# Gated linear attention and two MLPs on one core: decay work passes two waits per mixing step, and squares queue behind the table functions

## The chip, the cores and the metric

The kernel runs on 1 core of a Trainium2 chip. The metric is the device time of one execution in microseconds (us). Before the change the median of 3 runs is 912.96 us (908.11 to 916.42). The profiled execution took 912.68 us, of which its trace covers a span of 910.9 us.

The engines are named as in the profile: PE is TensorE (its sequencer of weight loads is PEld), DVE is VectorE, ACT is ScalarE, POOL is GpSimd, SP is SyncE, which issues most DMAs.

## The reference

Inputs are 4 batches x 8 heads x 768 positions x 48 channels. The first part is a linear recurrence with a complex decay per position and channel; its output is fed through a token-mixing MLP, a channel MLP, a layer norm and a second channel MLP.

```python
mag = sqrt(a_re**2 + a_im**2);  s = minimum(mag, 0.999) / (mag + 1e-6)
a_re, a_im = a_re * s, a_im * s
for t in range(768):                     # per batch and head, state 48 x 48
    S_re, S_im = a_re*S_re - a_im*S_im + k[t] v[t]^T, a_re*S_im + a_im*S_re
    y[t] = q[t] @ S_re
x = y, heads side by side                # 4 x 768 x 384
u = x + (relu(x^T @ w_tok1) @ w_tok2)^T  # 768 -> 256 -> 768 over tokens
u = u + relu(u @ w_ch1) @ w_ch2          # 384 -> 1536 -> 384
out = u + relu(norm(u) * g @ m_ch1) @ m_ch2
```

## The kernel before

The recurrence is not stepped through. For each batch the decays are turned into cumulated magnitudes and angles, q and k are scaled by them, and each head becomes a few matmuls on chunks of 128 positions. So there are three kinds of work, each a Python generator, and a driver that takes turns between them:

- **Decay work** (`gen_E`, class `Piece`). A batch's 8 x 48 channels are 3 tiles of 128 partitions; each tile is worked in two pieces of 384 positions. A piece runs through the parts F (squares of both decay parts, L228, logarithms and exponentials, L198, magnitude), G (a scan), H (scaling of q and k), T1 (arctangent and a scan of the angle), T2 (sine and cosine) and T3 (products, L172 on VectorE, and the DMAs into the heads' stacked tiles `stk`, L338 and L339). The work is split over ScalarE (functions of `aj` and `t`) and VectorE (all recorded at L172). ScalarE holds one table of functions at a time: the helper `act` loads the logarithm table or the sine table (L196) when the kind changes and puts the first function of the new kind behind all functions of the old kind. `Piece.F` calls the squares directly, not through `act`, so nothing but its data says where they stand.
- **Heads** (`gen_P`). A head is transposes of k (L507), scores of 3 x 128 columns twice (L520), states (L547), outputs (L570 to L577 for heads of batches 3 and 4), with their evictions, splits into two 16-bit halves and sums of squares on ScalarE and VectorE. Three steps per head.
- **Mixing** (`gen_M`). Per batch: token mixing (`tok1`, two hid activations; `tok2`, six evictions at L721), then 4 passes of a channel MLP, 12 steps each. Each step is 9 matmuls 128x384 from `u`, one activation on ScalarE (L670, written to `hid`), its remainder on VectorE (L672), and 9 matmuls from `hid`. Token mixing of the next batch needs all eight heads of that batch.

The driver, at the end of `tile_kernel`, runs one mixing step, then `run_E(2200)`, then up to two head steps. `run_E` takes items of decay work until their costs sum to 2200 or until the generator yields "wait", a mark that the next item needs another engine's result. A piece has seven such marks, so a batch has 42, against 48 mixing steps. Heads are taken at most at half a step per mixing step, and not before the tile that they need. When 47 steps are done all heads of the next batch are run at once. Decay work of a tile also waits until a head has given up its `stk` tile. So decay work and heads of batch b+1 (and some decay work of b+2) lie beside the mixing of batch b.

What is written this way is then put into an order for each engine by a scheduler that follows data dependences and a timeline of its own; an instruction written late can stand early. Each engine works its own list strictly in that order.

There are 198 hid activations at L670 (48 in batch 1, 50 in each other batch), evenly spaced in the work; this document uses their number as a ruler. Numbers 49 and 50 are token mixing of batch 2, 99 and 100 of batch 3, 149 and 150 of batch 4.

Of the kernel before, what the change touches and what calls it, by code (L numbers as in the profile page):

```python
# [38 lines left out]
def tile_kernel(ctx: ExitStack, tc: tile.TileContext, a_in, qk_in, v_in, aq2_in, v2_in, wt_in, wm1_in, wm2_in, w64_in, g_in, c_in, out):  # L39
# [150 lines left out]
    def act(**k):  # L190
        s = "trig" if k["func"] in (AF.Sin, AF.Arctan) else "logs"
        if tab["set"] != s:
            with ExitStack() as gates:
                for x in tab["ops"]:
                    gates.enter_context(tc.issue_after(x))
                tab.update(set=s, load=A.preload_act_table_set(sets[s]).ins, ops=[])  # L196
        with tc.issue_after(tab["load"]):
            tab["ops"].append(A.activation(**k).ins)  # L198

    class Piece:  # L200

# [20 lines left out]
        def F(self):  # L222
            V = Rec()
            A_, B_, C_, D_ = self.t
            ar, ai, b = self.ar, self.ai, self.b
            c = 470 if self.n == 1 else 870
            yield "wait"
            A.activation(out=self.sq.rearrange("p (x s) -> p x s", x=2), in_=self.both, func=AF.Square)  # L228
            act(out=D_, in_=ar, func=AF.Ln)
            act(out=D_, in_=D_, func=AF.Exp, scale=-1.0, accum_out=acc())  # L230
            yield "wait"
            with after("go") if b == 1 and self.i == 0 and EGO else ExitStack():
                V.scalar_tensor_tensor(out=A_, in0=A_, scalar=TINY, in1=B_, op0=ALU.add, op1=ALU.add)
# [79 lines left out]
        def T3(self, qkt):  # L313
            V = Rec()
            A_, B_, C_, D_ = self.t
            b, i = self.b, self.i
            for y in (self.R, qkt):
                d = y[:, :, 2 * HB:2 * HB + 3]
                if self.hf == 0:
                    (A.activation(out=d, in_=self.h(self.dh), func=AF.Copy) if ACP else G.tensor_copy(out=d, in_=self.h(self.dh)))  # L320
                else:
                    if self.n == 2:
                        (A.activation(out=d[:, 0], in_=self.dh[:, 0:3], func=AF.Copy) if ACP else G.tensor_copy(out=d[:, 0], in_=self.dh[:, 0:3]))
                    (A.activation(out=d[:, self.n - 1, 0:2], in_=self.dh[:, 3 * self.n - 3:3 * self.n - 1], func=AF.Copy) if ACP else G.tensor_copy(out=d[:, self.n - 1, 0:2], in_=self.dh[:, 3 * self.n - 3:3 * self.n - 1]))
                    G.memset(d[:, self.n - 1, 2:3], 0.0)
            for k in range(self.n):
                hf = k if self.n == 2 else self.hf
                qk = qkt[:, k, 0:2 * HB].rearrange("p (x s) -> p x s", x=2)
                V.tensor_tensor(out=self.R[:, k, 0:2 * HB].rearrange("p (x s) -> p x s", x=2), in0=qk, in1=pair(self.h(A_)[:, k]), op=ALU.mult)
                yield 870  # L330
                V.tensor_tensor(out=qk, in0=qk, in1=pair(self.h(B_)[:, k]), op=ALU.mult)
                r = 0
                while r < P:
                    h, d0 = divmod(i * P + r, D)
                    m = min(D - d0, P - r)
                    if (b, h) not in stk:
                        stk[b, h] = shared() if b == 0 and h >= 2 else ap.tile([2 * D, 2, 2 * HB + 3], F32, tag="stk", name="stk", bufs=NSTK)
                    nc.sync.dma_start(out=stk[b, h][d0:d0 + m, hf], in_=self.R[r:r + m, k])  # L338
                    nc.sync.dma_start(out=stk[b, h][D + d0:D + d0 + m, hf], in_=qkt[r:r + m, k])  # L339
                    r += m  # L340
                yield 870

# [105 lines left out]
    def gen_P(alt):  # L448
# [30 lines left out]
        for n, (b, h) in enumerate(heads):  # L479
# [17 lines left out]
                dr = ap.tile([P, 2, DM], F16, tag="hid", name="dr", bufs=NHID).rearrange("p a b -> p (a b)").bitcast(F32)[0:2 * D, 0:NCH * D].rearrange("p (e c) -> p e c", c=NCH)  # L497
            else:
                dr = ap.tile([2 * D, D, NCH], F32, tag="dr", name="dr", bufs=1)
            A.activation(out=dr.rearrange("p e (y c) -> p e y c", y=2), in_=kq[:, :, 2 * HB:].unsqueeze(1).to_broadcast([2 * D, D, 2, 3]), func=AF.Copy)  # L500
            tr = ps_(2)
            Gv = tr[0:96, 0:NCH * D]
            y = None
            for half in range(2):
                if half == 0:
                    for c in range(5):
                        T.transpose(tr[:, c * 96:(c + 1) * 96], qc(c, 1), eye[0:96, 0:96])  # L507
                    kTc = A.activation(out=kT, in_=tr[:, 0:480].rearrange("p (c d) -> p c d", c=5), func=AF.Copy, scale=(VS * SS if n in YS else 1.0) / (QS if n in QZ else 1.0))
                    if n in YS:
                        vh = ap.tile([P, S], F32, tag="dw", name="vh", bufs=NDW).bitcast(F16)  # L510
                        Uh = vh[0:2 * D, 2 * NCH * D:4 * NCH * D].rearrange("p (x c e) -> p x c e", x=2, c=NCH)
                        Uc = U.rearrange("p e c -> p c e")
                        vh = vh[:, 0:2 * NCH * D].rearrange("p (x c e) -> p x c e", x=2, c=NCH)
                        m = YS.index(n)
                        A.activation(out=vh[:, 0], in_=v, func=AF.Copy, scale=VS)
                        V.scalar_tensor_tensor(out=vh[:, 1], in0=v, scalar=VS, in1=vh[:, 0], op0=ALU.mult, op1=ALU.subtract)
                        A.activation(out=junk_p, in_=v, func=AF.Square, scale=VS, accum_out=qstat[:, m:m + 1])
# [7 lines left out]
                ev = V.tensor_tensor(out=sT[half], in0=sc[:, 0:3 * P].rearrange("p (c t) -> p c t", c=3), in1=pair(mask, 3), op=ALU.mult)  # L525
# [72 lines left out]
    def load_w(n):  # L598
        while len(raws) <= n:
            m = len(raws)  # L600
            raws[m] = load_raw(m, "w2" if m in (2, 3) or 8 <= m < 16 else "tw")

    def split_w(dst, n):

        load_w(min(15, n + 4) if 7 <= n < 12 else 3 if n < 2 else n + 1 if n < 27 else 27)
# [89 lines left out]
    def tok1_half(g, r1):  # L695
# [3 lines left out]
        for j in range(2):  # L699
            for tc_ in range(NCH):  # L700
                n, k = divmod(2 * tc_ + j, 3)
                w = tokv(0, n // 2)[:, n % 2]
                mm3(p[:, j], w[:, 0, k * P:(k + 1) * P], w[:, 1, k * P:(k + 1) * P], xh[:, tc_, cs], xl[:, tc_, cs], tc_ == 0, tc_ == 5)
            A.activation(out=r1[j][:, 0, cs], in_=p[:, j], func=AF.Relu, accum_out=hstat[:, n_h[0]:n_h[0] + 1])
            n_h[0] += 1
            fin['r1'] = V.scalar_tensor_tensor(out=r1[j][:, 1, cs], in0=p[:, j], scalar=0.0, in1=r1[j][:, 0, cs], op0=ALU.max, op1=ALU.subtract).ins

# [314 lines left out]
                    nc.sync.dma_start(out=out[c, :, bass.ds(bi * S + q * HB, HB)], in_=u[:, c])  # L1022


    st = {"phase": "", "alt": True, "e": 0, "p": 0, "pp": 0, "w": 0, "need": 0, "c": 0, "mk": 0}
    E, Pg, Wg, M = gen_E(), gen_P(lambda: st["alt"]), gen_W(), gen_M()

    e0 = []
# [21 lines left out]
    def run_E(budget, until=None):  # L1050

        if until is None and budget < 0:
            return
        while st["e"] < 3 * B and (until is None or st["e"] < until):
            if st["need"] > st["p"]:
                return
# [6 lines left out]
                else:  # L1063
                    st["e"] = x[1] * 3 + x[2] + 1
            elif x == "wait":
                if until is None:
                    return
            elif isinstance(x, str):
                st["phase"] = x
            else:  # L1070
                budget -= x
# [45 lines left out]
    st["alt"] = False  # L1117
    for b in range(B):
        k = 0
        while True:  # L1120
            if b == 0:
                run_W(max(need_w(k), int(k * W_RATE)))
# [156 lines left out]
```

## Time and profile before

| | before |
|---|---|
| median of 3 runs | 912.96 us (908.11 to 916.42) |
| profiled execution, its span | 912.68 us, 910.9 us |
| PE, DVE, ACT busy share | 90%, 69%, 67% |
| mean granted TensorE clock | 0.96 |

A busy share of PE counts matmuls whose ends overlap the next one's start, so 90% does not say how fast they follow each other. Shares are means over stages: decay work and heads lie beside the mixing of batches 1 to 3 and nothing of it beside that of batch 4. A stage's own rows say which engine holds it back.

### The profile page before, as it was taken

How to read it: one execution, taken by the hardware profiler on the slowest of the kernel's cores; microseconds unless marked ns; L12 is line 12 of the kernel's file. 1: busy time of each engine (PE TensorE's matmuls, PEld its weight loads, DVE VectorE, ACT ScalarE, POOL GpSimd, SP SyncE). 2: the span in 40 equal slices, each digit the busy share in tenths (PEclk: the TensorE clock that was granted, in tenths of full speed). 3: DMA queues.
4: the chain of work that ended last, by engine and by line, in shares of the span. 5: the costliest groups of instructions: out<-in, count | busy, mean ns of one | idle time of the engine just before them, and what ended most of it. 6: DMA issues, size and time to landing. Idle time of an engine off the chain costs nothing.

```text
span 910.9 us, 15777 instructions
## 1 busy us (share of the span) xinstructions
PE 816.8 (90%) x5802; PEld 551.3 (61%) x5802; DVE 631.2 (69%) x1094; ACT 606.2 (67%) x1631; POOL 97.8 (11%) x171
## 2 busy tenths in 40 slices
PE   0079898999989999999999988999999999999996
PEld 0068775555757676666567755666567766655563
DVE  6786479998888988426789987336889642364533
ACT  8787147785578996627879996627779934464642
POOL 0421020311011001000020103000020000011110
PEclk9977799999999899999999986999999999999999
DMA  8634684155742642101524141100403011465662
GB/s 302 190 105 125 169 296 140 53 157 153 218 155 68 196 139 82 48 2 45 147 60 145 41 129 47 53 14 14 131 27 117 27 37 60 143 203 196 201 223 97
DMA packets 41606, 108.28 MB, mean 119 GB/s; under 512 B 5904, under 2 KB 23824, under 8 KB 41520
## 3 DMA queue, kind: packets, MB, share of 16 engines
q1 hardware_dynamic: 31936, 56.72, 20.9%
q0 software_dynamic: 9584, 50.47, 17.3%
q8 instruction: 47, 0.77, 0.4%
q14 instruction: 39, 0.32, 0.1%
HBM read 77.20 MB, written 11.01 MB: 97 GB/s over the span
## 4 chain that ended last, share of the span: by engine, by line
PE 34%; ACT 6%; DVE 6%; SPq 2%; issue 1%; DMA 1%; DVEq 0%; ACTq 0%
PE m L663 10%; PE m L664 10%; PE m L662 10%; ACT t L198 1%; PE sc L520 1%; DVE t L172 1%; DVE qk L172 1%; ACT hid L670 1%; SPq L338 1%; SPq L339 1%; PE tr L547 1%; DVE aj L172 1%; DVE xc L780 1%; DMA stk<-t 1%; PE m L719 0%
## 5 line engine op out<-in xcount | busy, mean ns | idle before, releaser
L672 DVE SCALAR_TENSOR_TENSOR hid<-m,hid 128x384 f16<-128x384 f32 x198 | 109.4, 554 | 149.2 <-ACT hid L670 148.6
L662 PE MATMUL m<-u,w 128*128 128x384 f16 x576 | 188.1, 327 | 1.4 <-DVE u L722 0.8
L663 PE MATMUL m<-u,w 128*128 128x384 f16 x576 | 188.0, 326 | 0.0
L664 PE MATMUL m<-u,w 128*128 128x384 f16 x576 | 188.0, 326 | 0.0
L670 ACT ACTIVATE hid<-m 128x384 f16<-128x384 f32 x198 | 95.5, 483 | 138.5 <-PE m L664 137.8
L663 PE MATMUL m<-hid,w 128*128 128x384 f16 x540 | 177.6, 329 | 3.0 <-DVE hid L672 2.7
L664 PE MATMUL m<-hid,w 128*128 128x384 f16 x540 | 177.6, 329 | 0.0
L662 PEld LDWEIGHTS <-w 128*128 128x128 f16 x1176 | 116.1, 99 | 84.6 <-issue 15.2
L664 PEld LDWEIGHTS <-w 128*128 128x128 f16 x1176 | 116.6, 99 | 80.2 <-issue 10.6
L663 PEld LDWEIGHTS <-w 128*128 128x128 f16 x1176 | 116.3, 99 | 76.3 <-issue 4.9
L662 PE MATMUL m<-hid,w 128*128 128x384 f16 x540 | 131.6, 328 | 9.1 <-ACT hid L670 8.3
L172 DVE SCALAR_TENSOR_TENSOR t<-t 128x384 f32<-128x384 f32 x80 | 44.1, 555 | 16.7 <-ACT t L228 12.0
L520 PE MATMUL sc<-stk 96*128 96x128 f32 x300 | 46.1, 288 | 1.6 <-DVE r L525 1.6
L595 POOL DMA_DIRECT2D raw<-in_wm x48 | 25.6, 534 | 174.9 <-DVE sq L640 83.2
L520 PEld LDWEIGHTS sc<-stk 96*128 96x128 f32 x300 | 41.5, 200 | 3.7 <-DVE r L525 1.8
L641 ACT ACTIVATE sq<-sq 128x768 f16<-128x768 uint8 x28 | 23.6, 843 | 28.4 <-DVE sq L640 28.4
L507 PE MATMUL m<-cst,stk 96*128 96x96 f32 x10 | 2.1, 348 | 45.0 <-DMA stk<-qk 45.0
L198 ACT ACTIVATE t<-t 128x384 f32<-128x384 f32 x80 | 40.6, 514 | 0.3
L615 ACT ACTIVATE w<-raw 128x768 f16<-128x768 f32 x28 | 25.3, 904 | 22.2 <-DVE raw L613 22.2
L670 ACT ACTIVATION_READ_ACCUMULATOR hid<-m 128x1 f32 x198 | 38.5, 195 | 0.0
L172 DVE TENSOR_TENSOR qk<-qk,t 128x768 f32<-128x768 f32 x40 | 38.1, 955 | 0.5
L612 DVE SCALAR_TENSOR_TENSOR pad<-raw 128x768 uint8<-128x768 uint8 x28 | 29.0, 1034 | 11.6 <-DMA raw<-in_wm 9.3
(281 smaller groups left out, 1713.7 us busy)
## 6 DMA issues: line engine op xcount, KB each, us to landing
raw<-in_wm POOLq DMA_DIRECT2D x48, 768.0 KB, 4.8
qk<-in_qk SPq DMA_DIRECT2D x23, 384.0 KB, 4.0
aj<-in_a SPq DMA_DIRECT2D x9, 768.0 KB, 5.0
stk<-t SPq DMA_DIRECT2D x40, 144.6 KB, 3.2
stk<-qk SPq DMA_DIRECT2D x40, 144.6 KB, 3.0
raw<-in_wt SPq DMA_DIRECT2D x6, 768.0 KB, 4.5
v<-in_v SPq DMA_DIRECT2D x32, 144.0 KB, 2.4
x_d<-xc SPq DMA_DIRECT2D x24, 192.0 KB, 3.5
```

The source lines that it names most:

```text
L172: r = getattr(nc.vector, n)(*a, **k)
L198: tab["ops"].append(A.activation(**k).ins)
L520: last = T.matmul(sc[:, (c % 3) * P:(c % 3 + 1) * P], qc(c, 1), qc(c, 0), start=True, stop=True)
L595: (nc.sync if n < NSY else nc.gpsimd).dma_start(out=raw.bitcast(U8), in_=w_src[n].bitcast(U8)[:, 3:3 + 8 * S])
L612: V.scalar_tensor_tensor(out=pad[0].bitcast(U8).rearrange("p (a b) -> p a b", b=4)[:, :, 3], in0=byte, scalar=3, in1=byte, op0=ALU.logical ...
L615: wact[n] = A.activation(out=dst[:, :, 0], in_=w, func=AF.Copy, scale=WS).ins
L641: A.activation(out=t[:, HB:2 * HB].bitcast(F16), in_=bad_, func=AF.Copy, accum_out=wstat[:, n:n + 1])
L662: T.matmul(out_, wh, xh_, start=first, stop=False)
L663: T.matmul(out_, wh, xl_, start=False, stop=False)
L664: T.matmul(out_, wl, xh_, start=False, stop=last)
L670: A.activation(out=hl[:, 0], in_=p, func=AF.Relu, accum_out=hstat[:, n_h[0]:n_h[0] + 1])
L672: last[:] = [V.scalar_tensor_tensor(out=hl[:, 1], in0=p, scalar=0.0, in1=hl[:, 0], op0=ALU.max, op1=ALU.subtract).ins]
```

## The change

Two things. In `run_E` the "wait" marks are counted: while batch 1 is mixed the first mark still ends the turn, while batches 2 to 4 are mixed the second one does (`EW = 2`). And the squares of a piece of batches 2 to 4 are put, on ScalarE, behind the last table function written before them (`GSQ = 1`). The other new names (`HOLD`, `AHOLD`, `DQ`, `RW2`, `AHEAD`, `EBA`, `KA`) have values with which the code does what it did. All counts of instructions stay.

```diff
@@ class Piece, F
             yield "wait"
-            A.activation(out=self.sq.rearrange("p (x s) -> p x s", x=2), in_=self.both, func=AF.Square)
+            with tc.issue_after(tab["ops"][-1]) if b and GSQ else ExitStack():
+                A.activation(out=self.sq.rearrange("p (x s) -> p x s", x=2), in_=self.both, func=AF.Square)
             act(out=D_, in_=ar, func=AF.Ln)
...
@@ run_E
+        waits = EW if st["bb"] else 1
         while st["e"] < 3 * B and (until is None or st["e"] < until):
...
             elif x == "wait":
-                if until is None:
+                waits -= 1
+                if until is None and waits <= 0:
                     return
...
     for b in range(B):
         k = 0
+        st["bb"] = b
...
-            run_E(EB if b else EB0 if k <= KE else EB1)
+            run_E((EBA if k <= KA else EB) if b else EB0 if k <= KE else EB1)
...
+EW = 1
+EBA = 2200
+KA = 0
+GSQ = 1
...
 NSTK = 5
+EW = 2
```

The first place is ScalarE just before token mixing of batch 3. Before, 43 rows stand between the hid activations 98 and 99; they begin with these. `kT`, `qh`, `hl`, `xh`, `junk` belong to four heads, two of batch 3 and two of batch 4, `t` to two decay pieces.

```order
L670 ACTIVATE hid_6723,hstat_90<-m1_6713 128x384
L244 ACTIVATE t_7290<-t_7290,bias_83 128x384
L508 ACTIVATE kT_7296<-tr_7300 128x480
L517 ACTIVATE junk_111,qstat_93<-v_5731 128x288
L537 ACTIVATE qh_6384<-stk_6164 96x768
L198 ACTIVATE t_7291<-t_7291 128x384
L254 ACTIVATE first_107<-t_7290 128x3
L531 ACTIVATE junk_111,qstat_93<-hl_6335 128x384
```

Now the activations 98, 99 and 100 stand almost together (lines are shifted by 1 to 6; L676 is the hid activation).

```order
L676 ACTIVATE hid_6988,hstat_90<-m1_6978 128x384
L513 ACTIVATE kT_7721<-tr_7725 128x480
L534 ACTIVATE hl_7222<-r_7220 128x384
L676 ACTIVATE hid_7053,hstat_90<-m1_7013 128x384
L676 ACTIVATE hid_7056,hstat_90<-m1_7014 128x384
```

Of 43 rows between two activations 2 are left; the decay work and the heads have gone to earlier and later places.

The second place is ScalarE right behind activation 100, where `tok2` evicts six results (L721, now L727). Before:

```order
L670 ACTIVATE hid_6802,hstat_90<-m1_6760 128x384
L721 ACTIVATE u_1051<-m1_6819 128x384
L725 ACTIVATE junk_111,ustat_91<-u_1051 128x384
L721 ACTIVATE u_1051<-m1_6837 128x384
...
L721 ACTIVATE u_1051<-m1_6855 128x384
...
L475 ACTIVATE xh_109<-y_7379 128x6x48
```

Now, with squares of the decays at L231 and table functions at L199:

```order
L676 ACTIVATE hid_7056,hstat_90<-m1_7014 128x384
L504 ACTIVATE dr_8067<-stk_7346 96x288
L534 ACTIVATE hl_7234<-r_7232 128x384
L727 ACTIVATE u_1051<-m1_7073 128x384
L731 ACTIVATE junk_111,ustat_91<-u_1051 128x384
L231 ACTIVATE t_7433<-aj_68 128x768
L199 ACTIVATE t_7433<-aj_68 128x384
L199 ACTIVATE t_7434<-aj_68 128x384
L727 ACTIVATE u_1051<-m1_7091 128x384
L199 ACTIVATE t_7433,rstat_87<-t_7433 128x384
```

The last tile of batch 4's decays, which stood between activations 123 and 134, now starts here, between the evictions: 20 of its rows come before activation 101. One batch earlier it is alike: behind activation 50 now stand the end of the second tile of batch 3 and the start of its third, which were behind activations 69 to 79.

The third place is TensorE where it turns to token mixing of batch 3. Before, it runs parts of two heads of batch 4 there and then the whole output of the last head of batch 3 (`y_6562`), which token mixing (`tokw`) needs.

```order
L577 MATMUL y_6400<-vh_6325,qh_6384 128x48
L507 MATMUL tr_7421<-cst_81,stk_7240 128x96 x5
L520 MATMUL sc_7323<-stk_7237 128x128 x3
L547 MATMUL tr_7421<-v_6478,kT_7417 96x48 x5
L520 MATMUL sc_7432<-stk_7240 128x128 x3
...
L570 MATMUL y_6562<-vh_6491,hl_6501 128x48
...
L662 MATMUL m1_6759<-xh_109,tokw_6075 128x384
```

Now the mixing step's matmuls run straight into those with the token weights.

```order
L670 MATMUL m2_6417<-hid_6964,w2_2769 128x384
L669 LDWEIGHTS w2_2769
L669 MATMUL m2_6418<-hid_6964,w2_2769 128x384
L670 MATMUL m2_6418<-hid_6964,w2_2769 128x384
L668 LDWEIGHTS tokw_6564
L668 MATMUL m1_7013<-xh_109,tokw_6564 128x384
```

The last head of batch 3 has moved forward: its output is now evicted behind activation 93.

## Rows read from the trace of the kernel before

**Rows 1.** Page, parts 1 and 2: busy us (share) and instructions; granted clock in 40 slices.
```profile
PE 816.8 (90%) x5802; PEld 551.3 (61%) x5802; DVE 631.2 (69%) x1094; ACT 606.2 (67%) x1631; POOL 97.8 (11%) x171
PEclk9977799999999899999999986999999999999999
```
**Rows 2.** Windows, cut at hid activations 25, 50, 60, 95, 100, 110, 150, 198: busy us, clock.
```profile
0.00:228.09 228.09, 162.07 (x1047) 119.17 (x1048) 181.12 (x288) 148.93 (x344) 42.76 (x73) 0.92 0.54 169
228.09:357.69 129.60, 123.87 (x915) 90.16 (x914) 114.11 (x194) 105.51 (x274) 14.13 (x32) 0.96 0.48 140
357.69:397.13 39.44, 38.55 (x311) 25.36 (x310) 16.91 (x32) 20.84 (x66) 0.54 (x1) 1.00 0.19 59
397.13:526.48 129.35, 126.45 (x927) 83.37 (x926) 103.88 (x183) 102.45 (x285) 9.36 (x18) 1.00 0.27 78
526.48:565.50 39.02, 32.62 (x261) 22.70 (x259) 31.19 (x56) 33.48 (x101) 8.43 (x8) 0.74 0.29 83
565.50:601.42 35.92, 35.83 (x283) 22.62 (x279) 11.78 (x21) 18.69 (x62) 1.12 (x2) 1.00 0.17 53
601.42:749.41 147.99, 145.91 (x1130) 96.06 (x1128) 101.27 (x180) 105.24 (x306) 6.60 (x10) 1.00 0.18 54
749.41:899.47 150.06, 148.56 (x928) 90.04 (x929) 66.51 (x133) 70.50 (x201) 14.90 (x27) 1.00 0.52 168
```
**Rows 3.** Timeline of ACT: hid activations 98 (start, duration) and 99 with the wait before.
```profile
539.47 0.48 ACT L670 ACTIVATE hid<-m 128x384 f16<-128x384 f32 x1
...
565.01 0.49 ACT L670 ACTIVATE hid<-m 128x384 f16<-128x384 f32 x1 [5.27 <-PE m L664]
```
**Rows 4.** Waits of PE from 526.48 to 565.5: us, times, longest.
```profile
PE y L570 <- ACT junk L477: 2.0, 2, 1.6
PE m L662 <- ACT hid L670: 1.9, 1, 1.9
PE m L662 <- ACT xh L475: 1.1, 1, 1.1
PE m L663 <- DVE xl L476: 0.5, 1, 0.5
```
**Rows 5.** Windows, columns as in rows 2: TensorE's slow stretch at the end of batch 2's mixing.
```profile
540.00:561.60 21.60, 17.02 (x126) 12.56 (x126) 20.82 (x38) 19.65 (x60) 8.23 (x6) 0.53 0.13 42
```
**Rows 6.** Timeline of PE at full clock: 128x384 and 128x128 matmuls, one behind the other.
```profile
566.24 0.32 PE L662 MATMUL m<-tokw,hid 128*128 128x384 f16 x1
566.40 0.32 PE L663 MATMUL m<-tokw,hid 128*128 128x384 f16 x1
566.56 0.33 PE L664 MATMUL m<-tokw,hid 128*128 128x384 f16 x1
...
567.21 0.22 PE L719 MATMUL m<-eye_h,xh 128*128 128x128 f16 x1
567.26 0.22 PE L719 MATMUL m<-eye_h,xl 128*128 128x128 f16 x1
```
**Rows 7.** Page, part 5, and lines by form from 357.69 to 899.47: ACT, busy us, mean ns.
```profile
L198 ACT ACTIVATE t<-t 128x384 f32<-128x384 f32 x80 | 40.6, 514 | 0.3
L228 ACT ACTIVATE t<-aj 128x768 f32<-128x768 f32 x8 | 6.7, 842 | 7.6 <-DMA stk<-t 7.5
L721 ACT ACTIVATE u<-m 128x384 f16<-128x384 f32 x18 | 8.8, 489 | 6.6 <-PE m L719 6.6
```
**Rows 8.** Windows, columns as in rows 2: hid activations 35 to 40.
```profile
275.95:310.56 34.61, 32.84 (x232) 24.64 (x231) 32.10 (x58) 31.75 (x81) 3.17 (x11) 0.90 0.43 124
```
**Rows 9.** Timeline of ACT: hid activations 50, 51, then 100, 101.
```profile
357.69 0.47 ACT L670 ACTIVATE hid<-m 128x384 f16<-128x384 f32 x1
...
371.94 0.47 ACT L670 ACTIVATE hid<-m 128x384 f16<-128x384 f32 x1
...
565.50 0.49 ACT L670 ACTIVATE hid<-m 128x384 f16<-128x384 f32 x1
...
576.21 0.47 ACT L670 ACTIVATE hid<-m 128x384 f16<-128x384 f32 x1
```
**Rows 10.** Timeline of ACT: a load of the table and the function behind it.
```profile
471.82 1.28 ACT L196 ACT_TABLE_LOAD   x1
473.12 0.94 ACT L198 ACTIVATE t<-aj 128x384 f32<-128x384 f32 x2
```
**Rows 11.** Windows, columns as in rows 2: hid activations 80 to 95, and 20 us of it.
```profile
463.85:526.48 62.63, 60.56 (x515) 43.58 (x513) 57.80 (x103) 59.24 (x169) 4.32 (x10) 1.00 0.31 91
500.00:520.00 20.00, 20.00 (x177) 15.02 (x176) 19.54 (x35) 19.97 (x61) 3.34 (x7) 1.00 0.15 42
```

More of the change, by code (lines that the diff above doesn't have):

```diff
@@ L174, in g @@
                     e0.append(r.ins)
+                    fin["V", len(e0) - 1] = r.ins
                 return r
@@ L198, in act @@
             tab["ops"].append(A.activation(**k).ins)
+            fin["A", len(e0) - 1] = tab["ops"][-1]
     class Piece:
@@ L338, in T3 @@
                     nc.sync.dma_start(out=stk[b, h][d0:d0 + m, hf], in_=self.R[r:r + m, k])
-                    nc.sync.dma_start(out=stk[b, h][D + d0:D + d0 + m, hf], in_=qkt[r:r + m, k])
+                    (nc.gpsimd if (b, i) in DQ else nc.sync).dma_start(out=stk[b, h][D + d0:D + d0 + m, hf], in_=qkt[r:r + m, k])
                     r += m
@@ L499, in gen_P @@
                 dr = ap.tile([2 * D, D, NCH], F32, tag="dr", name="dr", bufs=1)
-            A.activation(out=dr.rearrange("p e (y c) -> p e y c", y=2), in_=kq[:, :, 2 * HB:].unsqueeze(1).to_broadcast([2 * D, D, 2, 3]), func=AF.Copy)
+            with after(AHOLD.get(n)):
+                A.activation(out=dr.rearrange("p e (y c) -> p e y c", y=2), in_=kq[:, :, 2 * HB:].unsqueeze(1).to_broadcast([2 * D, D, 2, 3]), func=AF.Copy)
             tr = ps_(2)
@@ L507, in gen_P @@
                         T.transpose(tr[:, c * 96:(c + 1) * 96], qc(c, 1), eye[0:96, 0:96])
-                    kTc = A.activation(out=kT, in_=tr[:, 0:480].rearrange("p (c d) -> p c d", c=5), func=AF.Copy, scale=(VS * SS if n in YS else 1.0) / (QS if n in QZ else 1.0))
+                    with after(AHOLD.get(n)):
+                      kTc = A.activation(out=kT, in_=tr[:, 0:480].rearrange("p (c d) -> p c d", c=5), func=AF.Copy, scale=(VS * SS if n in YS else 1.0) / (QS if n in QZ else 1.0))
                     if n in YS:
@@ L524, in gen_P @@
                     sT.append(ap.tile([P, 3, P], F32, tag="sT", name="sT", bufs=NST))
-                ev = V.tensor_tensor(out=sT[half], in0=sc[:, 0:3 * P].rearrange("p (c t) -> p c t", c=3), in1=pair(mask, 3), op=ALU.mult)
+                with after(HOLD.get((n, half))):
+                  ev = V.tensor_tensor(out=sT[half], in0=sc[:, 0:3 * P].rearrange("p (c t) -> p c t", c=3), in1=pair(mask, 3), op=ALU.mult)
                 if n in YS:
@@ L600, in load_w @@
             m = len(raws)
-            raws[m] = load_raw(m, "w2" if m in (2, 3) or 8 <= m < 16 else "tw")
+            raws[m] = load_raw(m, "w2" if m in RW2 else "tw")
     def split_w(dst, n):
-        load_w(min(15, n + 4) if 7 <= n < 12 else 3 if n < 2 else n + 1 if n < 27 else 27)
+        load_w(min(27, AHEAD(n)))
         if not pad:
@@ L703, in tok1_half @@
                 mm3(p[:, j], w[:, 0, k * P:(k + 1) * P], w[:, 1, k * P:(k + 1) * P], xh[:, tc_, cs], xl[:, tc_, cs], tc_ == 0, tc_ == 5)
-            A.activation(out=r1[j][:, 0, cs], in_=p[:, j], func=AF.Relu, accum_out=hstat[:, n_h[0]:n_h[0] + 1])
+            fin["relu", g, j] = A.activation(out=r1[j][:, 0, cs], in_=p[:, j], func=AF.Relu, accum_out=hstat[:, n_h[0]:n_h[0] + 1]).ins
             n_h[0] += 1
@@ L1022, in general @@
                     nc.sync.dma_start(out=out[c, :, bass.ds(bi * S + q * HB, HB)], in_=u[:, c])
-    st = {"phase": "", "alt": True, "e": 0, "p": 0, "pp": 0, "w": 0, "need": 0, "c": 0, "mk": 0}
+    st = {"phase": "", "alt": True, "e": 0, "p": 0, "pp": 0, "w": 0, "need": 0, "bb": 0, "c": 0, "mk": 0}
     E, Pg, Wg, M = gen_E(), gen_P(lambda: st["alt"]), gen_W(), gen_M()
@@ L1082, in run_P @@
             run_E(0, until=tiles_for(st["p"]))
+            for key in (HOLD.get((st["p"], 0)), HOLD.get((st["p"], 1)), AHOLD.get(st["p"])):
+                while key and key not in fin:
+                    x = nxt(E, "E")
+                    if isinstance(x, tuple) and x[0] == "done":
+                        st["e"] = x[1] * 3 + x[2] + 1
             st["pp"] += 1
@@ L1180 @@
 PADB = 0
+HOLD = {}
+AHOLD = {}
+RW2 = (2, 3) + tuple(range(8, 16))
+AHEAD = lambda n: min(15, n + 4) if 7 <= n < 12 else 3 if n < 2 else n + 1
+DQ = ()
+EW = 1
+EBA = 2200
+KA = 0
+GSQ = 1
 PIPE = 0
```

## The prediction

> **What bounds the kernel now.** I read the page's busy shares first, then the stretches between hid activations, then the waits inside the worst one. The shares [rows 1] say only that PE is the engine to watch: 816.8 us of busy time in a span of 910.9, DVE and ACT some 630 and 610. The clock line shows a dip to 6 in the 25th slice and to 8 in the 24th; that is where I looked closer.
>
> The stretches [rows 2] are cut at hid activations, so that the same work can be compared before and after; I call them 1 to 8. To judge them I need PE's work at full clock. Matmuls of 128x384 start 0.16 us apart when nothing holds them, those of 128x128 0.056 apart [rows 6]; counting each stretch's matmuls with such spacings gives 115, 39, 123, 25, 35, 144 and 148 us for stretches 2 to 8. Against the lengths: stretch 8 (150.1), 3 (39.4) and 6 (35.9) are PE's own work to within 2 us. Stretch 2 is 14 over, stretch 4 is 6, stretch 7 is 4, and stretch 5, 39 us long, is 14 over. So PE bounds nearly everything after 400 us, except for stretch 5, the end of batch 2's mixing.
>
> Stretch 5 in detail. Hid activations 98 and 99 start 25.5 us apart [rows 3]; ACT works through the 43 rows between them, with a wait only at the end. PE waits there for ACT's evictions and for activation 98 [rows 4], its granted clock is 0.53 (the lower of its levels, 1.2 GHz) from 540.0 to 561.6, and DVE and ACT are busy 20.8 and 19.7 us of these 21.6 [rows 5]. Heads and decay work came late and all at once; token mixing of batch 3 had to wait for the last head. The stretches before it (3) and after it (6) have ACT busy for only half the time: 20.8 of 39.4 and 18.7 of 35.9 us.
>
> **The change, part by part.** Neither part adds or removes an instruction. EW = 2 makes the driver write decay work earlier; its tiles are then ready earlier, and so heads are too. GSQ holds squares (0.84 us each [rows 7]) behind the table functions written before them, on the same engine, so it adds no wait for another engine. What they do to time is where the load stands. I went through both orders and gave each row the mean duration of its line in the trace, with the total set to each engine's busy time. For the kernel before this gives ACT 107, 21, 104, 35, 18 and 105 us in stretches 2 to 7, where the trace has 105.5, 20.8, 102.5, 33.5, 18.7 and 105.2 [rows 2]: the count is good to 2 us. For the changed order it gives
>
> ACT 107, 47, 118, 6.5, 47, 68;
> DVE 108, 36, 110, 9, 36, 71 (before 109, 14, 102, 31, 11, 99);
> PE 116, 40, 127.5, 19, 41, 139.
>
> So 29 us of ACT work leave stretch 5 and 37 leave stretch 7; 27 go to stretch 3, 29 to stretch 6, 13 to stretch 4. Of PE's own work, 6 us of heads leave stretch 5 and 5 leave stretch 7, for stretches 4 and 6. The sum goes by the largest load of a stretch plus what waits have cost there so far:
>
> Stretch 1, 228.1 us: DVE's load falls from 184 to 181, two early squares leave ACT; the rest of the start hangs on loads and the first tile, which do not move. I take 0, between -4 and +3.
>
> Stretch 2, 129.6 us: loads as before. A peak flattens (the load between activations 35 and 40, 34.6 us long [rows 8], falls from 32 to 26 us on ACT), and another rises between 45 and 50 (19 to 24). I take -2, between -8 and +4.
>
> Stretch 3, 39.4 us: ACT now has 47 us for 40 of PE. Between activations 50 and 51, 14.25 us apart [rows 9], it gets 18.7 instead of 10. PE can run about one step (2.9 us) ahead of ACT, so not all of it shows: 46, +7. Bounds: 41 if the work hides behind PE, 51 if the clock also falls.
>
> Stretch 4, 129.35 us: PE's work rises from 123 to 127.5, and with the 5 us over it that the layer norm and evictions cost now, 132.5: +3, between -1 and +12.
>
> Stretch 5, 39.0 us: PE 19, ACT 6.5, DVE 9, no head in the way of token mixing: 19.5 us, the slow clock gone with the wait: -19.5, at worst -15.
>
> Stretch 6, 35.9 us: ACT 47 for 41 of PE; between activations 100 and 101, 10.7 us apart [rows 9], ACT gets 19, of which 11 are decay work (11 functions of 0.51 us [rows 7], two squares, seven smaller ones and four read-outs), between the evictions. 46 us, +10, bounds 41 and 52.
>
> Stretch 7, 148.0 us: only PE is left, 139 us, plus 4 for the layer norm as now: 143, -5, between -9 and 0. Stretch 8 has no decay work and no heads: 0.
>
> Sum: -2 + 7 + 3 - 19.5 + 10 - 5 = -6.5. From the profiled time of 912.68 us (1.8 over its span, 0.3 under the median) that is **906 us**.
>
> If a square is placed too early it waits for the DMAs of T3 to free its tile `t`. Before, such waits cost ACT 7.5 us in all from 357 us on [rows 7], in stretches where ACT had time to spare. SP's queue gets its DMAs of T3 earlier too, but the stretches that receive them have few. Both I take as 0; in stretch 3 and 6 that cover is thinner, and 3 us each are inside the bounds.
>
> One rule speaks against the change. ACT's loads of a function table take 1.28 us, and the function behind starts 0.02 us later [rows 10]. Two of them move into stretch 3 and two into stretch 6, and at 1.3 us each they are in the loads above. The Trainium skill (ScalarE: Activation LUTs, What ACT_TABLE_LOAD costs) adds some 1.38 us of draining to every such switch. By that, an estimate, the four would cost 5.5 us more and the sum would be 912. The trace here shows no such drain.
>
> **The rivals.** *ACT's new load hides* (faster). For it: from 500 to 520 us ACT was busy for 19.97 us, and PE still had its full clock and was busy throughout; between activations 80 and 95, 62.6 us apart, ACT had as much to do as PE (62 us each by the count), and that was the time they took [rows 11]. Against it: in stretches 3 and 6 the load is beyond PE's, and ACT works in order, so hid activations stand behind table functions. Then stretches 3, 4 and 6 take 41, 129 and 42: 12.5 us less, **894 us**.
>
> *The pile-up moves to the starts of batches 2 and 3* (slower). One mechanism: ACT saturated in stretches 3, 4 and 6, PE short of hid activations, and its clock at the lower level for some 20 us in stretch 3 and 6 as it was in [rows 5]. There, stretch 5 was 4 us longer than its largest load (39.0 against 35); that makes 51 us of each, +5 twice. Stretch 4, with three engines then loaded almost alike (127.5, 118, 110), would lose as much as stretch 2 does with 115, 107 and 109, which is 14 instead of 5: +9. **925 us.** It decides where PE waits for ACT long enough in stretch 3 and 6 to lose its clock; in stretch 5 that was with 17.0 us of PE busy in 21.6. The Trainium skill (TensorE: Matmul & The Clock Gate, HAM oscillation — how this bites in real kernels) says that pauses between groups of matmuls can bring the slow clock back, group after group; by that, this rival.
>
> *Only stretch 4 loses* what the ends gain: 915 us. *The order is changed but the chip sees nothing of it*, because decay work waits for heads and DMAs and not for its place: 913 us. Against that, in stretch 5 ACT and DVE hardly wait at all [rows 5].
>
> **How the numbers follow.** My forecast has 0.45, with its own range of 899 to 913; the hiding rival 0.25; the pile-up 0.15; stretch 4 alone 0.10; nothing 0.05. About 1% (9 us) is what a measurement of this kernel can tell from no change. Faster than 904: nearly all of the hiding case and a third of mine, 0.39. Slower than 922: most of the pile-up, 0.12. Within 1%: 0.49. The range of 8 in 10 goes from the faster rival to just short of the slower one, 890 to 922.
>
> **What would show it.** In the changed kernel's profile, hid activations 95 to 100 should be about 20 us apart from first to last at a clock of 1.00, and no wait of PE for a head before token mixing of batch 3. 50 to 60 and 100 to 110 should take 46 us each, with ACT near full, and waits of PE for L676's activation or for `tok2`'s evictions. 110 to 150 should take 143. I am wrong if 50 to 60 stays near 40, or if the clock falls there, or if stretches 1 and 2, which I hold still, move by more than 5 us.

## The result, and the profile after

The changed kernel takes **901.97 us** (median of 13 runs, 898.99 to 911.08) against 910.96 us of the kernel before (13 runs, 908.11 to 916.42). The ratio on record is 0.9919, 95% interval 0.9895 to 0.9943 (the two medians alone give 0.9901, inside it): 0.8% less, where 906 us from a profiled execution of 912.68 had been forecast, 0.7% less. The profiled execution took 905.98 us, its span is 904.0 us.

The page of the changed kernel, parts 1 and 2 (as [rows 1]):

```profile
PE 809.5 (90%) x5802; PEld 547.5 (61%) x5802; DVE 630.7 (70%) x1094; ACT 604.1 (67%) x1631; POOL 95.1 (11%) x171
PEclk9977869999999999999999999999999999999999
```

The dip in the 24th and 25th slice is gone; PE is busy for 7.3 us less. The windows of the changed kernel, cut at the same hid activations as [rows 2], with the same columns (length, then busy us of PE, PEld, DVE, ACT and POOL, then the granted clock, the DMA share and GB/s):

```profile
0.00:226.44 226.44, 162.94 (x1042) 120.55 (x1043) 179.33 (x283) 146.06 (x339) 40.98 (x72) 0.90 0.55 171
226.44:358.92 132.48, 124.11 (x929) 90.30 (x928) 111.49 (x191) 106.72 (x272) 12.99 (x27) 0.97 0.48 140
358.92:405.03 46.11, 40.70 (x327) 26.20 (x327) 37.79 (x67) 44.23 (x128) 7.34 (x12) 1.00 0.36 108
405.03:537.43 132.40, 128.85 (x1023) 87.03 (x1022) 111.03 (x198) 113.73 (x326) 13.79 (x21) 1.00 0.25 72
537.43:556.26 18.83, 18.83 (x127) 11.99 (x126) 10.34 (x19) 6.84 (x17) 0.00 (x0) 1.00 0.37 95
556.26:603.64 47.38, 43.98 (x371) 29.29 (x370) 37.90 (x65) 44.70 (x132) 3.58 (x10) 1.00 0.31 91
603.64:742.45 138.81, 138.58 (x1049) 90.33 (x1047) 71.96 (x132) 70.83 (x225) 1.55 (x2) 1.00 0.10 32
742.45:892.48 150.03, 148.55 (x928) 90.03 (x929) 66.46 (x133) 70.44 (x199) 14.89 (x27) 1.00 0.52 168
```

| stretch | 1 | 2 | 3 | 4 | 5 | 6 | 7 | 8 | 2 to 8 |
|---|---|---|---|---|---|---|---|---|---|
| before, us | 228.1 | 129.6 | 39.4 | 129.35 | 39.0 | 35.9 | 148.0 | 150.1 | 671.4 |
| forecast | 228.1 | 127.6 | 46 | 132.5 | 19.5 | 46 | 143 | 150.1 | 664.7 |
| after | 226.4 | 132.5 | 46.1 | 132.4 | 18.8 | 47.4 | 138.8 | 150.0 | 666.0 |

Stretches 2 to 8 lost 5.3 us. Stretch 5 halved and is now PE's alone (18.83 busy of 18.83); stretch 7 gave 9.2; stretches 3 and 6 took 18 back. The clock is 1.00 from stretch 3 on. Waits of PE in stretch 3 of the changed kernel, then in stretch 6 (total us, times, longest):

```profile
PE m L668 <- DVE u L728: 3.6, 3, 1.7
PE m L668 <- DVE hid L678: 1.1, 1, 1.1
PE m L668 <- ACT hid L676: 0.9, 1, 0.9
```
```profile
PE m L668 <- DVE u L728: 1.5, 2, 1.1
PE sc L525 <- DVE r L531: 1.2, 1, 1.2
PE m L668 <- ACT hid L676: 0.6, 1, 0.6
```

L728 is the remainder that VectorE takes of a `tok2` eviction after L727 on ACT. The timeline of ACT between hid activations 50 and 51 of the changed kernel (start, duration, line, tiles) shows what stands among those evictions:

```profile
364.78 0.48 ACT L727 ACTIVATE u<-m 128x384 f16<-128x384 f32 x1
365.15 0.61 ACT L199 ACTIVATE t<-t,bias 128x384 f32<-128x384 f32 x1
365.78 1.28 ACT L197 ACT_TABLE_LOAD   x1
367.07 0.94 ACT L199 ACTIVATE t<-aj 128x384 f32<-128x384 f32 x2
367.92 0.51 ACT L731 ACTIVATE junk<-u 128x384 bf16<-128x384 f16 x1
368.33 0.18 ACT L731 ACTIVATION_READ_ACCUMULATOR junk<-u 128x1 f32 x1
368.42 0.51 ACT L269 ACTIVATE t<-t 128x384 f32<-128x384 f32 x1
368.84 0.47 ACT L727 ACTIVATE u<-m 128x384 f16<-128x384 f32 x1
```

Two evictions are 4.06 us apart, with a table load, three table functions and a square of the decays between them.

Three windows of the changed kernel, hid activations 50 to 51, 51 to 60 and 100 to 101 (columns as above):

```profile
358.92:377.09 18.17, 13.83 (x139) 10.27 (x139) 17.87 (x33) 17.48 (x46) 5.61 (x7) 1.00 0.19 62
377.09:405.03 27.94, 26.87 (x190) 15.94 (x189) 19.92 (x35) 26.75 (x84) 1.72 (x5) 1.00 0.47 138
556.26:576.47 20.21, 17.51 (x167) 12.83 (x166) 16.03 (x31) 17.68 (x53) 1.31 (x4) 1.00 0.45 137
```

PE's idle time stands between 50 and 51 (4.3 us) and between 100 and 101 (2.7); from 51 to 60 PE is busy for 26.9 of 27.9 us although ACT is nearly full as well.

### The profile page after: what moved, and what is told of

It reads as the page before. It is cut to its first block, busy times and chain, and to the rows that moved or that the text cites. A ratio compares the mean times of both kernels' runs of the same rounds, so it can differ in the third digit from the quotient of the medians.

```text
span 904.0 us, 15736 instructions
## 1 busy us (share of the span) xinstructions
PE 809.5 (90%) x5802; PEld 547.5 (61%) x5802; DVE 630.7 (70%) x1094; ACT 604.1 (67%) x1631; POOL 95.1 (11%) x171
## 3 DMA queue, kind: packets, MB, share of 16 engines
q0 software_dynamic: 9584, 50.47, 17.4%
## 4 chain that ended last, share of the span: by engine, by line
PE 43%; ACT 7%; DVE 6%; DMA 2%; issue 1%; SPq 0%; DVEq 0%; ACTq 0%
PE m L669 13%; PE m L670 13%; PE m L668 13%; ACT t L199 2%; DMA stk<-t 1%; PE sc L525 1%; DVE t L172 1%; PE tr L553 1%; DVE hid L678 1%; ACT hid L676 1%; DVE qk L172 1%; DVE qh L544 0%; ACT junk L731 0%; DVE xc L786 0%; PE tr L803 0%
## 5 line engine op out<-in xcount | busy, mean ns | idle before, releaser
L669 PE MATMUL m<-hid,w 128*128 128x384 f16 x540 | 176.4, 327 | 6.3 <-DVE hid L678 5.9
L676 ACT ACTIVATE hid<-m 128x384 f16<-128x384 f32 x198 | 95.4, 482 | 122.5 <-PE m L670 121.8
L670 PE MATMUL m<-hid,w 128*128 128x384 f16 x540 | 176.3, 327 | 0.0
L668 PE MATMUL m<-hid,w 128*128 128x384 f16 x540 | 127.8, 326 | 6.9 <-ACT hid L676 6.9
L172 DVE SCALAR_TENSOR_TENSOR t<-t 128x384 f32<-128x384 f32 x80 | 44.3, 555 | 20.7 <-ACT t L231 15.0
L511 PE MATMUL m<-cst,stk 96*128 96x96 f32 x10 | 2.1, 347 | 46.1 <-DMA stk<-qk 46.1
L199 ACT ACTIVATE t<-t 128x384 f32<-128x384 f32 x80 | 40.8, 515 | 0.5 <-DVE t L172 0.3
L277 POOL TENSOR_TENSOR pstat<-aj,t 128x3 f32<-128x3 f32 x20 | 27.0, 1352 | 119.1 <-DVE t L172 80.2
L676 ACT ACTIVATION_READ_ACCUMULATOR hid<-m 128x1 f32 x198 | 38.6, 195 | 0.0
```

The lines of the kernel that those rows point to most:

```text
L277: (nc.vector if ACP else G).tensor_tensor(out=pc, in0=n_end, in1=w_end, op=ALU.mult)
L668: T.matmul(out_, wh, xh_, start=first, stop=False)
L669: T.matmul(out_, wh, xl_, start=False, stop=False)
L670: T.matmul(out_, wl, xh_, start=False, stop=last)
L676: A.activation(out=hl[:, 0], in_=p, func=AF.Relu, accum_out=hstat[:, n_h[0]:n_h[0] + 1])
```

## Two theories of the gain, and the experiments

From hid activation 25 on PE's idle time did not fall: length less busy time, summed over stretches 2 to 8, is 19.6 us in [rows 2] and 22.4 after. So my **first theory** was the clock: what was gained is the time in which PE ran at the lower level in stretch 5 ([rows 5], clock 0.53). The **rival**: ACT's rows set the length of stretch 5, and a slow PE only filled time that it would have waited in. For stretches 3 and 6 there were two readings as well: ACT's sum sets them (the forecast's), or the place of the decay rows among the evictions does.

Kernels are compared with the kernel before on the same chip, and by their profiled executions from hid activation 25 to 198 (671.4 us before), since stretch 1 varies from one execution to the next (at the end).

### Which of the two parts does it

**e1_gsq_alone**
```diff
-EW = 2
+EW = 1
```


> The changed kernel with EW back to 1: the squares queue behind the table functions, the driver passes one wait as before. Load theory: what counts is the load of ScalarE and TensorE per stretch, and EW = 2 moves it. By the count over the order stretch 5 (hid activations 95 to 100) keeps 36 us of ScalarE work for 24 of TensorE, stretch 3 keeps 23; so stretch 5 stays near 39 us, stretch 3 near 40, and the whole is 907 to 913 us against some 911 of the kernel before. Rival (early squares wait for the DMAs of T3 and hold up ScalarE; GSQ is what gains): 901 to 904 us.

Measured: 914.9 us against 911.22, ratio 1.0053 (1.0031 to 1.0074); 681.6 us from 25 to 198. The squares' part alone costs time, more than either reading had expected (907 to 913, or 901 to 904). In the profile stretch 5 stays at 39.1 us, and the cost is in stretch 6, 44.5 us for 35.9.

**e2_ew_alone**
```diff
-GSQ = 1
+GSQ = 0
```


> The changed kernel with GSQ = 0: two waits per mixing step, squares placed as their data allow. Load theory: by the count ScalarE has 41 us in stretch 3 instead of 47 and the rest is as in the changed kernel, so 898 to 904 us, stretch 5 near 19 us. Rival (GSQ is what gains): 909 to 912 us, and waits of ScalarE's squares for DMAs of stk of more than 5 us in the stretches 3 to 6.

Measured: 901.48 us, ratio 0.9899 (0.9876 to 0.9923); 665.8 us from 25 to 198, stretches 3, 5 and 6 at 46.1, 18.8 and 46.6. The second wait does all of it; with it, the squares' part neither gives nor costs.

### What set stretch 5

**e5_fill**, on the kernel before
```diff
+                if n in (24, 25):
+                    warm(4, sc)
...
+            if 95 <= n_h[0] < 100:
+                for _ in range(20):
+                    T.matmul(p[:, HB:HB + P], eye_h, kick[:, 0:P], start=True, stop=True)
             hid[k] = relu_split(p[:, 0:HB])
```


> The kernel before, with TensorE given work whose result nobody reads: twenty 128x128 matmuls (about 0.05 us each) after the first layer of each of the last five hidden tiles before hidden activation 100, and four 128x384 ones ahead of each half of the scores of heads 24 and 25, some 8 us at the full clock. ScalarE's row order moves a little: 57 rows stand between hidden activations 95 and 100 where there were 70. If what the change saved in the fifth stretch is the clock (TensorE went idle behind ScalarE, fell to 0.53 and then did the rest slowly), the granted clock of 95 to 100 stays near 1.0 and the stretch is shorter although work was added: from 39 to 32 to 36 us, and the time from hidden activation 25 on falls by 3 to 7 us. If ScalarE's queued rows set that stretch by themselves, the stretch stays at 37 to 40 us whatever the clock, and the time does not fall.

Measured: 909.83 us against 909.29, ratio 1.0013 (0.9981 to 1.0045); 672.3 us from 25 to 198. Stretch 5 read alone (30.7 us) seems to bear the clock theory out. But 13 ScalarE rows had moved to before hid activation 95, and 90 to 95 grew from 20.7 to 28.7. Taken together, hid activations 90 to 100, first of the kernel before, then of this one:

```profile
505.76:565.50 59.74, 53.08 (x438) 37.59 (x437) 51.11 (x90) 54.17 (x158) 11.01 (x14) 0.83 0.21 61
```
```profile
498.71:558.05 59.34, 56.12 (x550) 41.61 (x549) 51.35 (x90) 54.28 (x157) 10.43 (x14) 0.94 0.21 62
```

The same ScalarE work (54.2 us), 112 more matmuls, the clock at 0.94 instead of 0.83, and the same length. The clock theory had expected a shorter stretch. By itself this run doesn't refute it: the added matmuls need PE too (its busy time rose by 3.0 us), and they could have used up what the faster clock gave.

**e8_batch3_only**
```diff
-        waits = EW if st["bb"] else 1
+        waits = EW if st["bb"] == 2 else 1
```


> The changed kernel, in which the second wait is passed in the mixing steps of batch 3 alone and not in those of batch 2: ScalarE again has 70 rows between hidden activations 95 and 100, but 40 between 100 and 101, as the changed kernel. If the gain is the fifth stretch with its clock, it is gone: the fifth stretch is back at 37 to 40 us at a clock of 0.7 to 0.85, the sixth is 45 to 48, the seventh 139 to 145, and the time is that of the kernel before or up to 4 us above it. If it was the decay work ahead of the seventh stretch that gained, the time stays at 900 to 904.

Measured: 914.75 us against 909.29, ratio 1.0049 (1.001 to 1.0088); 681.6 us from 25 to 198, stretches 5, 6 and 7 at 39.5, 47.6 and 143.9. The gain is gone (5.5 us over the kernel before, where at most 4 was expected), as it should be if it lies in stretch 5. But the granted clock is 0.91, above the 0.7 to 0.85 that the expectation tied to the lost gain. Hid activations 95 to 100 of this kernel, and below it of e1_gsq_alone, which has the same rows in the same order up to there:

```profile
523.34:562.83 39.49, 28.14 (x258) 19.35 (x256) 31.88 (x56) 35.08 (x96) 9.19 (x9) 0.91 0.25 70
```
```profile
518.22:557.32 39.10, 29.25 (x257) 19.77 (x256) 31.72 (x56) 34.98 (x95) 9.17 (x9) 0.87 0.28 83
```

With [rows 2] that makes three profiles of two orders with 33.5 to 35.1 us of ACT work and 31.2 to 31.9 of DVE work in this stretch. At clocks of 0.74, 0.87 and 0.91 PE was busy for 32.6, 29.3 and 28.1 us, with about as many matmuls, and the lengths are 39.0, 39.1 and 39.5 us. A faster PE did not shorten the stretch.

**e9_fewer_squares**, on the kernel before: the sums of squares of heads 20 to 25 (a statistic of the range) are left out.
```diff
-                        A.activation(out=junk_p, in_=v, func=AF.Square, ...
+                        if n not in range(20, 26): A.activation(out=junk_p, in_=v, func=AF.Square, ...
```
(and likewise at lines 531, 540 and 553)

> The kernel before, without the sums of squares that ScalarE takes in heads 20 to 25 (lines 517, 531, 540 and 553), which leaves their part of the range statistic out: between hidden activations 95 and 100 ScalarE has 45 rows where there were 70, and nothing of the decays' plan is changed. If ScalarE's rows set the fifth stretch (39 us), it falls in proportion, to 25 to 29 us, near the 25.3 us of TensorE's work at the full clock, and the time from hidden activation 25 on falls by 8 to 13 us. If the stretch is TensorE's with its slow clock, it stays at 35 to 39 us.

Measured: 901.85 us against 910.11, ratio 0.9912 (0.9882 to 0.9943); 663.5 us from 25 to 198, 7.9 less than before, just under the 8 to 13 expected. Hid activations 95 to 100:

```profile
516.85:541.73 24.88, 23.08 (x217) 15.96 (x217) 21.91 (x40) 21.93 (x58) 0.78 (x3) 1.00 0.41 109
```

11.6 us of ACT's work left the stretch and 14.1 of its length, with the decays' code untouched. Hid activations 100 to 101 took 5.4 back (10.7 to 16.1 us): 7 rows moved in there, and PE waited 2.9 us for L722 (VectorE's remainder of a `tok2` eviction). This run too leaves a question open: the clock rose to 1.00 with the pauses gone, and DVE's work in the stretch fell as well, from 31.2 to 21.9 us.

What decides against the clock, beside the three profiles above, is who waited for PE in the kernel before. Waits of ACT from 526.48 to 565.5, and below them the longest of DVE (us, times, longest):

```profile
ACT hid L670 <- PE m L664: 5.3, 1, 5.3
```
```profile
DVE t L172 <- ACT t L228: 1.0, 2, 0.9
DVE vh L516 <- ACT vh L515: 1.0, 1, 1.0
DVE hid L672 <- ACT hid L670: 0.3, 1, 0.3
```

No row of DVE waited for PE there, and of ACT only activation 99, at the end. **The clock theory falls: the rows that ACT and DVE work through in order set stretch 5.** The slow clock there was a consequence that cost little: PE is last only at the very end, when ACT waits for token mixing [rows 3]; 12 of its matmuls start 0.32 us apart instead of 0.16, by which it cost some 2 us (an estimate) of the 14 that stretch 5 was over PE's work.

Which of the two engines sets it is not shown. The chain that ended last runs over DVE's rows almost throughout from 542.6 us until token mixing's second matmul line starts (L663; start, length):

```profile
557.04 0.47 DVE hl L529
557.51 0.38 DVE xl L476
557.94 0.48 PE m L663
```

DVE was busy for 20.8 of 21.6 us there, ACT for 19.7 [rows 5], and no run took work out of this stretch from one of them alone.

### What sets stretches 3 and 6

**e3_spread**
```diff
-EBA = 2200
-KA = 0
+EBA = 1100
+KA = 3
```


> The changed kernel with the first 3 mixing steps of batches 2 to 4 taking decay work for 1100 instead of 2200 (KA = 3, EBA = 1100). Load theory: by the count ScalarE has 36 us instead of 47 in stretch 3, 17 instead of 7 in stretch 5, TensorE stays the larger load there; stretch 3 falls from 46 to 41 or 43 us, stretch 5 stays near 20, the whole falls to 896 to 900 us against 902. Rival (the start of a batch is slow because decay work stands between the evictions of token mixing, whatever its amount): stretch 3 stays at 45 or more, 901 to 904 us.

Measured: 904.52 us against 911.22, ratio 0.9935 (0.9911 to 0.996); 667.5 us from 25 to 198. Hid activations 50 to 51 and 51 to 60:

```profile
350.50:368.68 18.18, 13.83 (x139) 10.27 (x139) 17.88 (x33) 17.48 (x47) 5.62 (x7) 1.00 0.20 69
368.68:395.31 26.63, 25.64 (x182) 15.48 (x181) 10.56 (x17) 17.40 (x58) 0.19 (x2) 1.00 0.49 143
```

From 51 to 60 ACT has 17.4 us of work instead of 26.8, and the stretch is only 1.3 us shorter, as much as PE's own work fell: it was PE's. Between 50 and 51 nothing moved, so nothing changed. The 896 to 900 us expected from a smaller sum were not reached.

**e4_more_scalar**
```diff
+                for _ in range(2 if b >= 2 else 0):
+                    A.activation(out=junk, in_=uh[:, c, ts], func=AF.Square)
```


> The changed kernel with two more squares on ScalarE (128x384, written to junk, 0.42 us each start to start) behind each of the six evictions of token mixing of batches 3 and 4: 5.0 us more of ScalarE in stretch 6, and the same 5.0 us at the start of stretch 8 where ScalarE is half idle. Load theory: stretch 6 is bounded by ScalarE and grows from 47.4 by 4 to 5 us, stretch 8 by 0 to 1; 906 to 908 us against 902. Rival (stretch 6 is long because of waits between engines, which leave ScalarE room): stretch 6 grows by at most 1 us, 902 to 903.

Measured: 899.22 us (4 runs) against 911.22, ratio 0.9898 (0.9851 to 0.9945); 665.4 us from 25 to 198. Hid activations 100 to 110, then 110 to 115:

```profile
547.42:594.34 46.92, 42.73 (x328) 28.47 (x327) 35.32 (x60) 44.01 (x126) 4.13 (x10) 1.00 0.25 77
594.34:609.01 14.67, 14.67 (x147) 9.38 (x146) 8.83 (x17) 12.41 (x41) 0.00 (x0) 1.00 0.41 107
```

The added squares pushed decay rows past 110, where PE has more to do than ACT, and stretch 6 did not grow. The time is below both expectations (906 to 908, 902 to 903). But ACT's sum in stretch 6 did not rise at all (44.0 us against 44.7), so the run does not test whether that sum sets the stretch. A stretch's sum is not fixed: the order gives way.

**e6_gate**, on the changed kernel
```diff
-        with tc.issue_after(tab["load"]):
+        with after('tok2'), tc.issue_after(tab["load"]):
...
+                if b in (1, 2):
+                    fin['tok2'] = lsq.ins
```
(`lsq` is the last square, L731, of `tok2`)

> The changed kernel, in which the table functions of a decay (logarithm, exponential, sine) are put behind the last square of the second token matmul of batches 2 and 3: of the 37 rows that ScalarE does between hidden activations 50 and 51, 15 are left there, of 39 between 100 and 101, 24; they stand after 55 and after 105 instead. If what the starts of batches 2 and 3 lose is that decay rows stand between the evictions that TensorE waits for, 50 to 51 falls from 18.2 to 14 to 15 us and 100 to 101 from 20.2 to 16 to 17, and the time from hidden activation 25 on by 4 to 8 us. If ScalarE's sum over these stretches sets them, stretches 3 and 6 stay at 45 to 48 us each, and the time stays.

Measured: **895.38 us** (889.44 to 897.86) against 909.29 of the kernel before, ratio 0.9836 (0.9797 to 0.9875); 660.2 us from 25 to 198, 5.4 less than e7_after_again on the same chip. Windows of 50 to 51, 100 to 101 and 60 to 95, and ACT's timeline between 50 and 51:

```profile
346.81:357.48 10.67, 9.98 (x85) 6.94 (x86) 4.45 (x8) 7.98 (x25) 1.13 (x2) 1.00 0.29 94
547.26:563.77 16.51, 16.01 (x168) 12.76 (x167) 9.70 (x19) 11.54 (x33) 1.32 (x4) 1.00 0.53 168
388.28:530.02 141.74, 133.83 (x1093) 89.96 (x1090) 132.35 (x236) 137.35 (x394) 18.59 (x29) 0.99 0.31 91
```
```profile
350.31 0.49 ACT L727 ACTIVATE u<-m 128x384 f16<-128x384 f32 x1 [0.17 <-PE m L725]
350.83 0.52 ACT L731 ACTIVATE junk<-u 128x384 bf16<-128x384 f16 x1
351.26 0.19 ACT L731 ACTIVATION_READ_ACCUMULATOR junk<-u 128x1 f32 x1
351.64 0.49 ACT L727 ACTIVATE u<-m 128x384 f16<-128x384 f32 x1 [0.19 <-PE m L725]
```

The evictions are 1.33 us apart, and ACT waits for PE ahead of each. 50 to 51 fell by 7.4 us against e7_after_again (expected 3 to 4: the heads' rows went out with the decays'), 100 to 101 by 4.0. What was put off shows between 60 and 95, now 9.3 us longer and full on ACT (137.4 of 141.7).

**e7_after_again** (the changed kernel, unedited)

> The changed kernel once more, beside the other three on one chip: 900 to 904 us, with stretches 3, 5 and 6 at 46, 19 and 47 us; whichever theory holds.

Measured: 901.62 us, ratio 0.9911 (0.9878 to 0.9943); 665.6 us from 25 to 198. Stretches 3, 5 and 6 at 46.1, 18.8 and 47.7.

**e10_gate_batch3**
```diff
-                if b in (1, 2):
+                if b == 2:
```


> The kernel with the gate of the run e6_gate at the start of batch 3 alone; at the start of batch 2 the decay's table functions stand as the changed kernel has them. If each gate saves by itself what its stretch showed, act 100 to 101 is 16 to 17 us and the sixth stretch 45 to 46 (the changed kernel: 20.5 and 47.7), the third stays at 46, and the time is 2 to 3 us under the changed kernel's, 898 to 900. If the first gate carried the whole 6 us (its rows moved out of the third stretch), the time stays at 901 to 902; if the first gate cost as much in the fourth stretch as it saved in the second and third, the time is 895 to 897 as with both.

Measured: 898.68 us against 910.11, ratio 0.9874 (0.9836 to 0.9912); 662.5 us from 25 to 198, stretch 6 at 44.7. Hid activations 100 to 101:

```profile
556.09:571.81 15.72, 15.72 (x163) 12.38 (x162) 9.22 (x18) 11.43 (x32) 1.32 (x4) 1.00 0.48 149
```

PE is busy throughout. The gate of batch 3 alone gives 3.0 us against e7_after_again in the profiles, and its time is in the 898 to 900 us expected of it. With the one of batch 2 on top it is another 2.3 us, which is no more than the scatter of one order (at the end), and the intervals of e6_gate and e10_gate_batch3 overlap: the first gate's own gain is not shown. In stretches 2 to 4 it nearly breaks even (309.7 us against 310.2 in e7_after_again); stretch 5 is 17.2 against 18.8.

**e11_gate_gsq0**
```diff
-GSQ = 1
+GSQ = 0
```


> Both gates of e6_gate, with the squares of later decays not queued behind the table functions (the second part of the change undone). If that part is worth nothing, as its run alone said, 893 to 898 us as with it.

Measured: 906.45 us against 910.11, ratio 0.9966 (0.9939 to 0.9993); 668.8 us from 25 to 198. A miss: with the gates the squares' part is worth 8.6 us (4.2 of them in stretch 2, 2.7 in stretch 7, 1.9 in stretch 5). Alone it cost some 10 us from 25 on in its profile, though only 3.7 by the medians of the runs, beside the second wait it did nothing, beside the gates it gains. What it does depends on the order around it; which rows make the difference was not settled.

The fastest version measured is e6_gate: both parts of the change and both gates.

## Why the prediction was right, and where it was not

- **Stretch 5**, the largest term (-19.5): measured -20.2. Its load counts were the right reason: ACT 35 us before and 6.5 after, DVE 31 and 9 (the traces have 33.5 and 6.84, 31.2 and 10.3), with PE's 19 left. Which of ACT and DVE held the stretch before stays open. "The slow clock gone with the wait" was true, and worth some 2 us by the estimate above.
- **Stretches 3, 4 and 6** (46, 132.5, 46): measured 46.1, 132.4 and 47.4, the sizes right. The rule behind 3 and 6, ACT's sum over the stretch, was not, so that 46 came out there in part by luck: e3 took 9 us of ACT's work out of 51 to 60 for 1.3 us of length. Of the time lost, the part that can be had back stands between 50 and 51 and between 100 and 101, where evictions queue behind decay rows (e6, e10). The rest is PE's moved heads: PE's busy time rose from 38.6 to 40.7 us in stretch 3 and from 35.8 to 44.0 in stretch 6.
- **Stretch 7** was mis-sized: -9.2 instead of -5. PE's own 139 us came out exactly (138.8). The step that failed is "plus 4 for the layer norm as now": with the decays gone PE is idle for 0.2 us there, where it was for 2.1 [rows 2]. Those 4 us went with the work beside it.
- **Stretch 2** was wrong: +2.9 instead of -2. Hid activations 35 to 40 fell from 34.6 [rows 8] to 29.5 us, as forecast, but the other peak gave it back, between 40 and 45 (23.1 to 28.7) rather than 45 and 50, where I had priced it below what it saved. The exchange goes with the squares' part: e1_gsq_alone has 30.2 and 26.5 us, e2_ew_alone 35.9 and 23.1. But stretch 2 scatters: seven profiles with the changed kernel's order up to hid activation 50 (also e1, e3, e4, e7, e8 and e10) have 130.4 to 133.0 us, three with the order before (also e5 and e9) 129.6 to 130.4, and e2_ew_alone, which leaves that order only at the end of the stretch, 132.9. So a loss here is not clear of the scatter; the forecast gain of 2 did not come.
- **Stretch 1**, taken as 0: 226.4 against 228.1, within the scatter of one order (at the end). Over all profiles the means are 222.0 us with the changed kernel's order up to hid activation 25 (8 of them) and 223.2 with the order before (5). Stretch 8 did not move.
- **Sum**: -6.5 forecast; -5.3 in stretches 2 to 8 of the profile, -7.4 us (-9.6 to -5.2) by the ratio of the runs. The misses of stretches 2 (+4.9) and 7 (-4.2) nearly cancel, which is luck. Two slips of the working are within 1 us: by its own lists 26 us of ACT's work go to stretch 3 and 14 to stretch 4, not 27 and 13, and what stretch 4 is over PE's work is 6 us in one place and 5 in the sum.
- **Table loads**: 1.28 us, and the function behind starts 0.01 us later (365.78 and 367.07 in the timeline above), as in [rows 10]. By the Trainium skill (ScalarE: Activation LUTs, What ACT_TABLE_LOAD costs), with its draining, the time had been estimated at 912; no drain is seen, and the sum without it held.
- **Squares and DMAs**, taken as 0: ACT's waits for `stk<-t` at the squares fell from 7.5 [rows 7] to 2.6 us.
- **Rivals.** "The load hides" (894) fails at 50 to 51 and 100 to 101. "The pile-up moves" (925) has its crowding there, but no slow clock: 1.00 in stretches 3 and 6. The rule that it leant on (the Trainium skill, TensorE: Matmul & The Clock Gate, HAM oscillation — how this bites in real kernels) did not come into play; PE paused between evictions in stretch 3 and kept its clock. Its price took stretch 5 as the pattern and so the slow clock for a loss; in stretch 5 that clock cost some 2 us. "Nothing" (913) fails: the stretches moved as the order said. "Only stretch 4 loses" (915) fails, since stretch 4 came out as forecast.

## What to carry to other kernels

Count each engine's work per stretch of the program before and after, and read a slow TensorE clock only together with who waits for TensorE there: in stretch 5 hardly anyone did, and the slow clock was a consequence. When work is moved ahead, look at what it lands between: moving decay rows (and heads' rows with them) from among the evictions that TensorE waits for shortened those places by 4 to 7 us here. What is put off has to fit somewhere else, though: behind batch 2's evictions the next stretch, where ScalarE became full, took 9.3 us back, and in the whole the two gates gave 5 to 6 us. Judge an experiment over a stretch wide enough that rows pushed over its edge are still inside.

## What was not expected

- The time to the first hid activation differs between profiled executions: 138.1 to 148.4 us over the kernels here, and 148.4, 140.4 and 142.4 us in three whose order up to there is the same (the changed kernel, e4_more_scalar, e7_after_again); with the order before it was 147.7 and, in e9_fewer_squares, 138.1. From 25 to 198 the changed kernel and its repetition agree within 0.5 us, but e1_gsq_alone and e8_batch3_only, with one order up to hid activation 100, have 337.0 and 340.0 us from 25 to 100, 2.6 of the difference in stretch 2. A change of a few us is therefore read from the stretch that it changes or from many runs.
- The clock fell in stretch 5 after a pause of 1.9 us of PE ([rows 4], [rows 5]), but pauses of up to 1.7 us in stretch 3 of the changed kernel left it at 1.00. Which pauses it answers to isn't settled here.
- About 2 us between the gain of the runs (-7.4 us by the ratio) and that of stretches 2 to 8 are left unexplained; they lie within the interval. By the medians alone it would be 4.
